# The order of twelve one-pass matmuls in a product that accumulates into two PSUM banks

## Chip, cores and metric

The kernel runs on one core of a Trainium2 chip. The time is the device time of one execution in microseconds, and the median of several executions is compared. TensorE is called PE in the profile, its weight loads PEld, VectorE DVE, ScalarE ACT, GpSimd POOL and SyncE SP. Matmul results go to PSUM, which has eight banks; a bank holds 512 fp32 values in each of 128 partitions.

## The reference

A linear attention block is followed by a two-layer feed-forward block with the gate serf(h) = h * erf(softplus(h)). Shapes: batch 8, 8 heads, sequence 576, head dimension 64; so 4608 tokens of width 512, and a hidden width of 2048.

```python
kv = np.einsum('bhsd,bhse->bhde', k, v)
out = np.einsum('bhsd,bhde->bhse', q, kv)
rms = np.sqrt(np.mean(out * out, axis=-1, keepdims=True) + 1e-06)
x = out / rms * g_norm            # then (B,H,S,D) -> (B*S, H*D)
h = x @ w_in
sp = np.maximum(h, 0.0) + np.log1p(np.exp(-np.abs(h)))
g = h * erf(sp)
return g @ w_out
```

Everything is fp32.

## The kernel before

The tokens are worked on in nine groups of 512: T = 0 to 7 take 512 of a batch entry's 576 tokens each, and T = 8 takes the 64 that each of the eight has left over. The hidden width is cut into 16 units of 128 (FC = 16), and four units make a batch (BATCH = 4). All orders are written out by hand; each engine works through its own queue in program order and waits at an instruction until what it needs is there. The waits of a matmul stand on its weight load.

**Two ways of multiplying.** For T = 0 a matmul takes plain fp32, which the array does in several passes. From T = 1 on (for w_out from the last batch of T = 1 on) a product is put together from one-pass matmuls on fp32r operands. Each operand is held in three forms: form 0, the upper part ("high"); form 1, the lower part ("low"); form 2, high and low combined with a scale ("both"). The function `product` uses two banks, n_ps and m_ps. For each of four chunks k of the contraction, forms 0 and 1 are accumulated into n_ps and form 2 into m_ps. That is twelve matmuls of 128x128 weights on 512 columns: eight into n_ps, four into m_ps. The value wanted is (SHIFT - 1) * n_ps + m_ps.

**Who calls `product`.** `hidden(T, f)` forms unit f of x @ w_in. Then ScalarE copies n_ps with the factor SHIFT - 1 into h (L1036 for T = 1, L1192 later), VectorE adds m_ps (L574), and ScalarE takes the softplus of h (L1050, L1197). `result(T, b, j, ...)` forms 128 tokens' share of g @ w_out for one batch; here VectorE takes both banks into the sum e (L1129 for the first batch of a group or L569 later for n_ps, L574 for m_ps). There are 244 products: 16 + 112 from `hidden` and 116 from `result`. In one of them, the very last, n_ps is cut into two column ranges in two banks (`cuts`).

**Which banks.** `pair_of_banks` hands out the two banks. With `turns=True` it goes round three pairs out of six banks (the two of ps_h, and o0 to o3 of ps_o), so a pair is used again three products later. In T = 1, `hidden` is called with `turns=False`, because o0 to o3 hold the output sums that `project` (L655) accumulates; all 16 products of T = 1 use the same two banks of ps_h. A tile in a bank can be written when the last reader of the tile before it there is done.

**The work around it in T = 1** (128.8 to 222.6 us). After a unit's product, four fp32 matmuls of `project` for the unit five before (LAG = 5) are issued, if there is one due: not between the first two units of T = 1, and not after the last three. In between stand pieces of attention for T = 2 (at_ps, L411 to L464). VectorE also makes the lower forms of the weights (w_lower, L561 and L564) from upper forms that ScalarE made (L558), multiplies gates (L902), and SP stores the weights' forms to DRAM. After the sixteenth product `held_sums` (L918, L949) finishes the last four units with products on o_ps and n_ps.

**The work from T = 2 on** (from 234.6 us). Each batch is four `hidden` products, then four `result` products for the batch before. The weights' forms come from DRAM (w_in_parts, w_out_parts). ScalarE makes the upper form of the gate (cut_upper, L534), and VectorE the other two in two halves of the tokens (cut_lower: L537 low, L540 both): half 0 after the first `hidden` of the next batch, half 1 after its fourth. Softplus, erf, the gate's multiplication (L1246) and one pair of heads' attention for the next group are spread over the batch. In the last batch there are only four `result` products.

Of the kernel before, what the change touches and what calls it, by code (L numbers as in the profile page):

```python
# [68 lines left out]
def kernel(  # L69
# [10 lines left out]
    nc = tc.nc  # L80
# [104 lines left out]
    def one(tiles, f):  # L185
        return tiles[f // 2][:, f % 2]

    def blocks_of(x):
        return x.rearrange("p (c f) -> p c f", c=KC)
# [102 lines left out]
    def w_next(what):  # L292
        i = w_at[what]
        if i < len(w_order):
            w_at[what] = i + 1
            {"load": load_w, "split": w_split, "join": w_join}[what](*w_order[i][1:])

    def weights():

        w_next("split")  # L300
        w_next("join")
        w_next("load")
# [275 lines left out]
    def pair_of_banks(*names, turns=True):  # L578
        pair = tuple(
            pool.tile([P, G], FP32, name=name, tag=tag)  # L580
            for name, (pool, tag) in zip(names, banks[:2])
        )
        if turns:
            banks.extend(banks[:2])
            del banks[:2]
        return pair

    def product(weights, moving, turns=True, cuts=()):


        n_ps, m_ps = pair_of_banks("n_ps", "m_ps", turns=turns)
        runs = [(n_ps, (0, 1), slice(0, G)), (m_ps, (2,), slice(0, G))]
        if cuts:
            n_ps = (n_ps, pair_of_banks("n_ps", "m_ps")[0])
            runs = runs[1:] + [(ps, (0, 1), cols) for ps, cols in zip(n_ps, cuts)]
        for ps, forms, cols in runs:
            for k in range(4):
                for form in forms:
                    nc.tensor.matmul(  # L599
                        ps[:, cols],  # L600
                        lhsT=weights(form, k),
                        rhs=moving(form, k)[:, cols],
                        start=(form == forms[0] and k == 0),
                        stop=(form == forms[-1] and k == 3),
                    )
        return n_ps, m_ps

    w_kept, w_new, w_now, w_held, w_places = {}, {}, {}, {}, {}
# [32 lines left out]
    def hidden(T, f, turns=True):  # L641

        w = w_now["in", f].pop(0).rearrange("p i (c f) -> p i c f", c=KC).bitcast(FP32R)
        x = x_forms[T]
        return product(lambda form, c: w[:, form, c], lambda form, c: x[form][:, c], turns)
# [330 lines left out]
    for n in range(FIRST * FC + 1):  # L976
# [31 lines left out]
        elif T < FIRST:  # L1008
# [11 lines left out]
            for i, c in blocks:  # L1020
                nc.tensor.matmul(  # L1021
                    plain[i],
                    lhsT=blocks_of(one(w_in_sb, i % FC))[:, c],
                    rhs=xT[T][:, c, :],
                    start=(c == 0),
                    stop=(c == KC - 1),
                )
        if T < FIRST:
# [22 lines left out]
            if n == FC - 2:  # L1051
# [8 lines left out]
                forms = late.tile([P, 3, KC, G], FP32R, name="x_forms0")  # L1060
# [57 lines left out]
    def result(T, b, j, g, w, cuts=()):  # L1118

        ps = product(  # L1120
            lambda form, f: g[j // 2][:, form, f, j % 2 * P : j % 2 * P + P],
            lambda form, f: w[f][:, form],
            cuts=cuts,
        )
        if b == 0:
            if j == 0:
                all_e = wide.tile([P, J, DM], FP32, name="e", tag="a")
                es.update((i, all_e[:, i]) for i in range(J))
            nc.vector.tensor_scalar(  # L1129
                out=es[j], in0=ps[0], scalar1=SHIFT - 1.0, scalar2=None, op0=ALU.mult  # L1130
            )
        elif not cuts:
            add_scaled(es[j], ps[0], SHIFT - 1.0)
        add(es[j], ps[1])
        for n_ps, cols in zip(ps[0], cuts):
            add_scaled(es[j][:, cols], n_ps[:, cols], SHIFT - 1.0)
            store(T, j, es[j], cols)
# [5 lines left out]
    for m in range(first_batch, batches + 1):  # L1143
# [3 lines left out]
        if T + 1 < NG:  # L1147
            todo = list(attention(T + 1, b, in_parts=last_))
            if b == 0:
                side = late_r if T % 2 == FIRST % 2 else late  # L1150
                forms = side.tile([P, 3, KC, G], FP32R, name=f"x_forms{(T + 1) % 2}")
# [73 lines left out]
        for j in range(J):  # L1225
            cuts = (slice(0, 3 * P), slice(3 * P, DM)) if m == batches and j == J - 1 else ()
# [59 lines left out]
```

## Time and profile before

| What | Value |
|---|---|
| Median of 3 runs | 902.89 us (902.69 to 903.44) |
| Span of the profiled execution, first to last instruction | 901.3 us |
| PE busy | 893.6 us, 99% |
| DVE busy | 766.7 us, 85% |
| ACT busy | 595.1 us, 66% |
| Granted TensorE clock | 0.999 |
| Matmuls of L599 into n_ps, from T = 2 on | 1,832 of 389 to 392 ns each (mean by group) |
| Matmuls of L599 into m_ps, from T = 2 on | 912 of 389 ns each |

For the profiled execution the span is its own time; the median of the runs is 1.6 us above it. Matmuls are pipelined: a row of 389 ns overlaps the next one, so the distance from start to start counts, not the length. In a timeline, the first column is the start in us from the span's start, the second the length, and in brackets stands how long the engine was idle before and what ended that. A run of like instructions stands in one row with its count. A list of waits gives who waited for whom: us in total, times, and the longest.

### The profile page before, as it was taken

What the parts mean: (1) busy time and instruction counts of PE and PEld (TensorE: products, weight loads), DVE (VectorE), ACT (ScalarE), POOL (GpSimd) and SP (SyncE); (2) the same over time, 40 slices, a digit from 0 to 9 for tenths busy, and PEclk for the clock granted to TensorE, in tenths of its full rate; (3) what the DMA queues carried; (4) which work ended last, traced back from release to release, by engine and by line L of the source; (5) the groups of instructions that cost most, each with busy time, mean ns of one, the idle gap of its engine ahead of it and who ended that gap; (6) DMA issues with size and microseconds to landing.
All of it is one profiled execution on the core that took longest, in us unless ns stands there. A gap on an engine that the chain in (4) does not pass through costs nothing.

```text
span 901.3 us, 13468 instructions
## 1 busy us (share of the span) xinstructions
PE 893.6 (99%) x4962; PEld 672.4 (75%) x4962; DVE 766.7 (85%) x1105; ACT 595.1 (66%) x789; POOL 4.7 (1%) x14
## 2 busy tenths in 40 slices
PE   8999999999999999999999999999999999999998
PEld 4444456666788888888888888888888888888887
DVE  5899978899799888888888888888888888886667
ACT  5976687777766666666766666666666666665552
POOL 2000000000000000000000000000000000000000
PEclk9999999999999999999999999999999999999999
DMA  9977418899699987988899979988897787778871
GB/s 285 295 224 226 108 73 319 305 341 355 233 384 355 347 301 258 382 308 297 273 361 336 320 248 335 365 300 292 286 341 273 270 304 309 286 282 323 317 263 51
DMA packets 136929, 259.89 MB, mean 288 GB/s; under 512 B 78816, under 2 KB 87264, under 8 KB 136864
## 3 DMA queue, kind: packets, MB, share of 16 engines
q1 hardware_dynamic: 136128, 258.09, 81.3%
q8 instruction: 39, 0.64, 0.3%
q10 hardware_dynamic: 544, 0.82, 0.3%
q14 instruction: 26, 0.21, 0.1%
q0 software_dynamic: 192, 0.13, 0.0%
HBM read 224.40 MB, written 34.60 MB: 287 GB/s over the span
## 4 chain that ended last, share of the span: by engine, by line
PE 96%; DMA 1%; DVE 1%; ACT 1%; issue 0%; SPq 0%; DVEq 0%
PE n_ps L599 50%; PE m_ps L599 25%; PE o_ps L655 9%; PE h_ps L1021 5%; PE at_ps L425 2%; PE at_ps L411 2%; PE n_ps L918 1%; PE at_ps L463 1%; PE at_ps L464 1%; DMA q_sb<-in_q_dram 1%; DMA w_raw<-in_moe_w_out_dram 1%; PE o_ps L918 0%; DVE w_e L276 0%; PE o_ps L722 0%; DVE w_in_sb L281 0%; PE ms_ps L729 0%
## 5 line engine op out<-in xcount | busy, mean ns | idle before, releaser
L599 PE MATMUL n_ps<-w_out_parts,g_forms 128*128 128x512 f32 (+1 forms) x936 | 230.7, 389 | 0.0
L599 PE MATMUL n_ps<-x_forms,w_in_parts 128*128 128x512 f32 x896 | 223.9, 392 | 0.0
L599 PEld LDWEIGHTS n_ps<-w_out_parts,g_forms 128*128 128x128 f32 x936 | 173.7, 188 | 35.3
L599 PEld LDWEIGHTS n_ps<-x_forms,w_in_parts 128*128 128x128 f32 x896 | 166.6, 188 | 35.3
L574 DVE TENSOR_TENSOR h<-m_ps,h 128x512 f32<-128x512 f32 x116 | 78.2, 687 | 60.3 <-PE m_ps L599 58.1
L599 PE MATMUL m_ps<-w_out_parts,g_forms 128*128 128x512 f32 x464 | 124.0, 389 | 0.0
L599 PE MATMUL m_ps<-x_forms,w_in_parts 128*128 128x512 f32 x448 | 119.7, 389 | 0.0
L1192 ACT ACTIVATE h<-n_ps 128x512 f32<-128x512 f32 x112 | 66.2, 594 | 75.1 <-PE n_ps L599 75.0
L1197 ACT ACTIVATE s<-h 128x512 f32<-128x512 f32 x112 | 68.3, 629 | 70.0 <-DVE h L574 70.0
L599 PEld LDWEIGHTS m_ps<-w_out_parts,g_forms 128*128 128x128 f32 x464 | 87.1, 188 | 18.5
L599 PEld LDWEIGHTS m_ps<-x_forms,w_in_parts 128*128 128x128 f32 x448 | 84.1, 188 | 17.5
L574 DVE TENSOR_TENSOR e<-m_ps,e 128x512 f32<-128x512 f32 x116 | 80.2, 692 | 15.2 <-PE m_ps L599 5.3
L655 PE MATMUL o_ps<-w_out_sb,h_sb 128*128 128x512 f32 x192 | 86.8, 595 | 0.0
L540 DVE SCALAR_TENSOR_TENSOR g_forms<-g_forms 128x1024 fp32r<-128x1024 f32 x58 | 71.1, 1225 | 2.0
L537 DVE TENSOR_TENSOR g_forms<-h,g_forms 128x1024 fp32r<-128x1024 f32 x58 | 70.6, 1217 | 1.2 <-ACT g_forms L534 1.1
L534 ACT ACTIVATE g_forms<-h 128x1024 fp32r<-128x1024 f32 x58 | 58.4, 1049 | 15.5 <-PE m_ps L599 11.1
L569 DVE SCALAR_TENSOR_TENSOR e<-n_ps,e 128x512 f32<-128x512 f32 (+1 forms) x89 | 60.4, 678 | 6.9 <-PE n_ps L599 6.9
L1246 DVE TENSOR_TENSOR h<-h,s 128x1024 f32<-128x1024 f32 x56 | 65.9, 1218 | 0.0
L655 PEld LDWEIGHTS o_ps<-w_out_sb,h_sb 128*128 128x128 f32 x192 | 35.5, 190 | 38.3 <-issue 36.9
L1021 PE MATMUL h_ps<-xT,w_in_sb 128*128 128x512 f32 x128 | 57.9, 596 | 1.1 <-DVE w_in_sb L281 1.1
L115 ACT ACT_TABLE_LOAD x43 | 55.2, 1283 | 0.8
L1220 ACT ACTIVATE s<-s 128x1024 f32<-128x1024 f32 x50 | 50.6, 1053 | 0.3
(148 smaller groups left out, 1018.7 us busy)
## 6 DMA issues: line engine op xcount, KB each, us to landing
w_out_parts<-w_out SPq DMA_DIRECT2D x116, 768.0 KB, 6.8
w_in_parts<-w_in SPq DMA_DIRECT2D x112, 768.0 KB, 6.7
w_in<-w_new SPq DMA_DIRECT2D x16, 768.0 KB, 4.9
k_sb<-in_k_dram SPq DMA_DIRECT2D x32, 288.0 KB, 5.9
v_sb<-in_v_dram SPq DMA_DIRECT2D x31, 288.0 KB, 5.8
w_raw<-in_moe_w_in_dram SPq DMA_DIRECT2D x16, 512.0 KB, 5.9
w_raw<-in_moe_w_out_dram SPq DMA_DIRECT2D x8, 1024.0 KB, 5.1
out_dram<-e SPq DMA_DIRECT2D x32, 256.0 KB, 3.8
```

Of the source, the lines that this page charges most:

```text
L115: nc.scalar.preload_act_table_set("softplus")
L534: nc.scalar.activation(high, x, AF.Copy, scale=1.0 + 2.0**-13)
L537: nc.vector.tensor_tensor(out=low, in0=x, in1=high.bitcast(FP32), op=ALU.subtract)
L540: nc.vector.scalar_tensor_tensor(out=both, in0=low.bitcast(FP32), scalar=SHIFT, in1=high.bitcast(FP32), op0=ALU.mult, op1=ALU.add,)
L569: nc.vector.scalar_tensor_tensor(out=out_, in0=ps, scalar=scale, in1=out_, op0=ALU.mult, op1=ALU.add)
L574: nc.vector.tensor_tensor(out=out_, in0=ps, in1=out_, op=ALU.add)
L599: nc.tensor.matmul(ps[:, cols], lhsT=weights(form, k), rhs=moving(form, k)[:, cols], start=(form == forms[0] and k == 0), stop=(form == fo ...
L655: nc.tensor.matmul(o_ps[j], lhsT=g[:, j * P : j * P + P], rhs=one(w_out_sb, f), start=(f == 0), stop=last,)
L1021: nc.tensor.matmul(plain[i], lhsT=blocks_of(one(w_in_sb, i % FC))[:, c], rhs=xT[T][:, c, :], start=(c == 0), stop=(c == KC - 1),)
L1192: nc.scalar.activation(h[:, i], n_ps, AF.Copy, scale=SHIFT - 1.0)
L1197: nc.scalar.activation(s[:, i], h[:, i], AF.Softplus)
L1246: nc.vector.tensor_tensor(out=part(h, half), in0=part(h, half), in1=part(s, half), op=ALU.mult)
```

## The change

The twelve matmuls of a product are put in another order. Before, the eight matmuls into n_ps come first (for each chunk form 0, form 1), then the four into m_ps. After, each chunk k has its three together: form 0 into n_ps, form 2 into m_ps, form 1 into n_ps. The operands, the banks, the start and stop marks and the number of matmuls stay as they are. A product with `cuts` keeps its order. Forms 0 and 1 of neighbouring chunks still follow each other in n_ps.

```diff
-        for ps, forms, cols in runs:
-            for k in range(4):
-                for form in forms:
-                    nc.tensor.matmul(
-                        ps[:, cols],
-                        lhsT=weights(form, k),
-                        rhs=moving(form, k)[:, cols],
-                        start=(form == forms[0] and k == 0),
-                        stop=(form == forms[-1] and k == 3),
-                    )
+        order = [(*run, k, form) for run in runs for k in range(4) for form in run[1]]
+        if not cuts:
+            order.sort(key=lambda one_: (one_[3], (0, 2, 1)[one_[4]]))
+        for ps, forms, cols, k, form in order:
+            nc.tensor.matmul(
+                ps[:, cols],
+                lhsT=weights(form, k),
+                rhs=moving(form, k)[:, cols],
+                start=(form == forms[0] and k == 0),
+                stop=(form == forms[-1] and k == 3),
+            )
         return n_ps, m_ps
```

## The prediction

> **What bounds the kernel now.** I read the page first (parts 1, 2, 4), then the list of what PE (TensorE) waits for, then timelines by engine, and last the starts of single matmuls.
>
> ```profile
> PE 893.6 (99%) x4962; PEld 672.4 (75%) x4962; DVE 766.7 (85%) x1105; ACT 595.1 (66%) x789; POOL 4.7 (1%) x14
> PEclk9999999999999999999999999999999999999999
> PE 96%; DMA 1%; DVE 1%; ACT 1%; issue 0%; SPq 0%; DVEq 0%
> ```
>
> TensorE is the bound: 96% of the chain that ended last, clock granted in full throughout. So there are two ways to move the time: another distance from matmul to matmul, or a wait on TensorE that isn't there now. Today there is next to none; its longest waits over the whole span are
>
> ```profile
> PE warm_ps L802 <- DVE ones L198: 1.4, 1, 1.4
> PE h_ps L1021 <- DVE w_in_sb L281: 1.1, 2, 0.7
> ...
> PE n_ps L918 <- ACT e L949: 0.2, 1, 0.2
> ```
>
> (total us, times, longest). Only the third lies after 128 us, where the changed products begin. A saving on DVE (VectorE) or ACT (ScalarE) would bring nothing; a delay there costs as soon as it reaches a bank or an operand that TensorE wants.
>
> **Distance between matmuls.** The change makes more neighbours differ in bank. The trace already holds both kinds side by side, in PE's timeline:
>
> ```profile
> 226.80 1.07 PE L918 MATMUL o_ps<-w_place,g_held 128*128 128x512 f32 x4
> 227.70 1.07 PE L918 MATMUL n_ps<-w_place,g_held 128*128 128x512 f32 x4
> 228.61 1.07 PE L918 MATMUL o_ps<-w_place,g_held 128*128 128x512 f32 x4
> 229.52 1.07 PE L918 MATMUL n_ps<-w_place,g_held 128*128 128x512 f32 x4
> ```
>
> The o_ps rows are four matmuls into four different banks, the n_ps rows two pairs, each pair into one bank. Start to start: 0.90, 0.91, 0.91 us for four, about 227 ns each, either way. In the starts of single matmuls after 258 us, an m followed by the next n takes 226.8 ns on average (178 pairs), an n followed by its m 226.9 (219), an m by an m 227.0 (661). A change of bank is free and brings nothing. Now to the count: of the 11 neighbourings inside a product one changes bank today (n8 to m1), 8 would afterwards (n m n n m n n m n n m n). 243 products are reordered, 7 x 243 = 1,701 neighbourings in all. The rows leave at most 1 ns on each, so 0 us, with bounds of -1.7 and +1.7. I take 0.
>
> Here two rules of the Trainium skill bear. "TensorE: Matmul & The Clock Gate", section "Back-to-back issue gap", gives N/2.4 + 2.5 ns, which is 216 ns for 512 columns, below the 227 of the rows. If that gap of about 11 ns were the price of one bank, an estimate by the page would be 1,701 x 11 = 18.7 us gained and 888 us; the page names no such cause, and the switching rows above show 227 too.
>
> **What moves: the end of n.** Today the eight n matmuls end 0.93 us before the four m matmuls. After the change n's last matmul is the product's twelfth and m's last the eleventh. ACT's copy of n (0.60 us) then starts 0.93 us later, and DVE's add of m (0.69), which needs that copy, begins when the copy ends: 0.6 us later than now wherever it waited for TensorE. In the result products DVE reads both banks itself; there the pair ends up to 0.87 us later. Second, m's first matmul moves from place 9 to place 2: its bank and its third operand (the "both" form) are wanted 1.6 us earlier.
>
> "Perfetto Trace Analysis", section "Matmuls", of the skill says that groups should rotate through banks so that the evacuation of one overlaps the matmuls of the next. Read strictly it speaks against this change: the copy of n lies under m's matmuls today and would lie under nothing of its own product. By that rule alone, exposed in each of 243 products, an estimate is 243 x 0.60 = 146 us. The rows decide where it is exposed.
>
> *Where banks don't rotate (16 products, 128.8 to 222.6 us).* They all use the same two banks (turns=False). Behind 12 of them stand 3.4 us of projection matmuls (o_ps L655), behind one 1.3 us of attention matmuls, behind the last 2.5 us of means and held sums: enough for 0.04 + 0.60 + 0.06 + 0.69 = 1.39 us of copy and add. Behind the products at 128.82 and 216.78 the next one follows at once:
>
> ```profile
> 131.06 1.09 PE L599 MATMUL m_ps<-x_both,w_new 128*128 128x512 f32 x4
> 131.99 0.42 PE L599 MATMUL n_ps<-x_high,w_new 128*128 128x512 f32 x1
> 132.24 0.40 PE L599 MATMUL n_ps<-x_low,w_new 128*128 128x512 f32 x1
> 132.47 0.39 PE L599 MATMUL n_ps<-x_high,w_new 128*128 128x512 f32 x1
> ```
>
> ```profile
> 131.26 0.60 ACT L1036 ACTIVATE h_sb<-n_ps 128x512 f32<-128x512 f32 x1 [0.76 <-PE n_ps L599]
> 132.25 0.69 DVE L574 TENSOR_TENSOR h_sb<-m_ps,h_sb 128x512 f32<-128x512 f32 x1 [2.72 <-PE m_ps L599]
> ```
>
> Today the copy ends at 131.86, under m's matmuls, and the next product's n starts at 131.99 unhindered. Afterwards: the product ends at 132.15, copy 132.19 to 132.79, add 132.85 to 133.54. The next product's first matmul must wait for the copy, its second (now m) for the add. A weight load that waited starts 0.05 us after its release and its matmul takes 0.11 us more than the usual 0.227 (copy end 230.77, matmul 230.82, next one 231.16). So the third matmul starts at 133.54 + 0.05 + 0.227 + 0.11 = 133.93 and not 132.47: 1.46 us. The other place is the same to 0.01 us (219.63, third at 220.12, then 221.57): 1.45 us. Together 2.9 us, all on the path.
>
> For the rest of this stage the nearest margins, from end of add to start of the second matmul of the next product, are 0.76 us (product at 212.19), 1.07 (205.95) and 1.23 (179.08). The first shrinks by 0.6 to 0.15. In the others a chain of ACT work in front (uppers, softplus, Ln, Exp, table loads) hands on the full 0.93 us, leaving 0.14 and 0.30. Cost 0; if I am wrong by 0.2 us on each, 0.5 us in all. What queues on DVE behind a later add (gates, w_lower and its DMAs on SP) serves the product after the next and has over 2 us.
>
> *The entry to the rotating stage.* The first product at 234.58 takes banks that held n_ps[2] and n_ps[3] of the held sums:
>
> ```profile
> 234.58 2.01 PE L599 MATMUL n_ps<-x_forms,w_in_parts 128*128 128x512 f32 x8
> 234.78 0.60 ACT L949 ACTIVATE e<-n_ps 128x512 f32<-128x512 f32 x1 [0.69 <-PE n_ps L918]
> 236.42 1.08 PE L599 MATMUL m_ps<-x_forms,w_in_parts 128*128 128x512 f32 x4
> ```
>
> The copy of n_ps[3] ends at 235.37; m wants that bank at 236.42 today, at 234.81 afterwards. Third matmul at 235.37 + 0.05 + 0.34 = 235.76, not 235.03: 0.73 us.
>
> *Rotating stage (227 products, three pairs).* A bank is wanted again three products (8.2 us) later. Margins from add to the second matmul three products on: 1.72 us once per ordinary batch, least 1.09 (product at 776.91). The shift of DVE, 0.6 to 0.87, fits in each, and it doesn't pile up: in the batch from 353.8 to 377.6 DVE idles 2.2 us, 1.34 of it in front of the fourth h add, where it waits for TensorE again and is back in step. Cost 0.
>
> *The last batch.* DVE works without a gap from 875.58, so the 0.59 us stays to the end:
>
> ```profile
> 890.24 1.22 DVE L540 SCALAR_TENSOR_TENSOR g_forms<-g_forms 128x1024 fp32r<-128x1024 f32 x1
> 891.63 1.98 PE L599 MATMUL n_ps<-w_out_parts,g_forms 128*128 128x512 f32 x8
> ```
>
> The third form is finished at 891.46, then at 892.05. Today it is used at place 9 (893.45); afterwards at place 2 (891.86). Third matmul at 892.05 + 0.05 + 0.34 = 892.44, not 892.09: 0.35 us. What follows (cut product, last store) is bound by TensorE and moves along.
>
> **Sum.** 1.46 + 1.45 + 0.73 + 0.35 = 4.0 us. The profiled execution spans 901.3 us, 1.6 below the median of 902.89; 905.3 of span gives 906.9 us.
>
> **Rivals.**
> 1. *Same bank costs something that single changes don't show* (the other side). If neighbours in one bank came down from 226.7 to the shortest distance of any pair in the trace, 224 ns, 1,701 x 2.7 = 4.6 us would come off: 906.9 - 4.6 = 902.3, no slower than now. It decides from 2.4 ns on each (4.0/1,701); to be faster by over 0.2% it takes 3.4 ns. For: 230 to 239 ns between the n matmuls of some products of the two-bank stage. Against: the four-bank rows at 227. 11%, of which 5% faster by over 0.2%.
> 2. *DVE falls behind in the rotating stage.* If its 0.87 us reached TensorE in each of 28 batches: 24 us, 931 us; if a third of it, 8 us, 915 us. For: DVE is busy 20.7 of 23.8 us in the batch from 330. Against: margins of 1.09 and more at each bank. 9%.
> 3. *TensorE's new waits are made good later*, because something else was late anyway. It could only be at 230.82, where TensorE now loses 0.4 us to ACT: 906.5. But that copy itself waits for TensorE (n_ps L918). 5%, inside the range.
>
> The forecast has 75%; with rival 3 that is 8 in 10. Range 904.9 to 909.0: below for 1.7 us of distance and 0.3 of noise, above for 1.7 and the 0.5 of thin margins. About what this kernel's measurement tells from no change is 0.2%, 1.8 us. Faster by more: 0.05, from rival 1. Within it: 0.08, the rest of rival 1 and 2% of the forecast's own lower edge. Slower: 0.87.
>
> **What would show it.** Right: waits of PE on DVE h_sb and h L574 at about 133 and 221 us, on ACT e L949 at 235, on DVE g_forms L540 at 892; 227 ns between matmuls elsewhere; DVE's idle time in front of the fourth h add of a batch shorter in total, never zero. Wrong: products of other than 2.72 us in the rotating stage (rival 1), or waits of PE on L574 or L569 once per batch (rival 2).

## The result, and the profile after

The median after the change is 906.56 us (906.46 to 906.95, 4 runs) against 902.86 us before (902.69 to 903.44, 4 runs: the three of the table above and one timed beside the new kernel): 1.0041 times as long, 95% interval 1.0028 to 1.0053. The change costs 3.7 us. The profiled execution took 906.61 us and spans 904.8 us, 3.5 more than before.

Parts 1, 2 and 4 of the page after:

```profile
span 904.8 us, 13218 instructions
...
PE 895.1 (99%) x4962; PEld 672.9 (74%) x4962; DVE 766.0 (85%) x1105; ACT 598.1 (66%) x789; POOL 4.7 (1%) x14
...
PEclk9999999999999999999999999999999999999999
...
PE 94%; DMA 2%; DVE 1%; SPq 1%; ACT 0%; issue 0%; DVEq 0%
```

TensorE is still the bound, with the same 4962 matmuls at full clock; DVE's busy time has not grown. What is new stands at the end of the list of PE's waits (its last six rows; total us, times, longest):

```profile
PE n_ps L600 <- ACT h_sb L1037: 0.7, 1, 0.7
PE n_ps L600 <- ACT h L1037: 0.7, 1, 0.7
PE m_ps L600 <- ACT e L950: 0.5, 1, 0.5
PE n_ps L919 <- ACT e L950: 0.2, 1, 0.2
PE m_ps L600 <- DVE h_sb L574: 0.2, 1, 0.2
PE m_ps L600 <- DVE h L574: 0.2, 1, 0.2
```

All but the fourth row, which is in the list of before too, are new. (Lines behind the change are one higher than before: L1037 is ScalarE's copy of n, L950 its copy of a held sum. L574, DVE's add of m, stands ahead of the change and keeps its number.) PE's timeline at the first place shows how one product hands over to the next:

```profile
131.70 0.39 PE L600 MATMUL n_ps<-x_low,w_new 128*128 128x512 f32 x1
132.77 0.50 PE L600 MATMUL n_ps<-x_high,w_new 128*128 128x512 f32 x1 [0.69 <-ACT h_sb L1037]
133.50 0.50 PE L600 MATMUL m_ps<-x_both,w_new 128*128 128x512 f32 x1 [0.23 <-DVE h_sb L574]
133.84 0.40 PE L600 MATMUL n_ps<-x_low,w_new 128*128 128x512 f32 x1
```

The two readers, in the timelines of ACT and then DVE:

```profile
132.12 0.60 ACT L1037 ACTIVATE h_sb<-n_ps 128x512 f32<-128x512 f32 x1 [1.72 <-PE n_ps L600]
```

```profile
132.75 0.69 DVE L574 TENSOR_TENSOR h_sb<-m_ps,h_sb 128x512 f32<-128x512 f32 x1 [3.31 <-ACT h_sb L1037]
```

The copy starts only when the whole product is over and ends at 132.72; n's next matmul starts 0.05 us later. The add ends at 133.44; m's next matmul starts 0.06 us later. The entry to the rotating stage, in PE's timeline and then ACT's:

```profile
237.17 0.39 PE L600 MATMUL n_ps<-x_forms,w_in_parts 128*128 128x512 f32 x1
238.02 0.50 PE L600 MATMUL m_ps<-x_forms,w_in_parts 128*128 128x512 f32 x1 [0.46 <-ACT e L950]
```

```profile
237.37 0.60 ACT L950 ACTIVATE e<-n_ps 128x512 f32<-128x512 f32 x1 [0.69 <-PE n_ps L919]
```

The copy of the last held sum ends at 237.97, and the m matmul that wants its bank starts at 238.02. The last batch, in PE's timeline and then DVE's:

```profile
894.72 0.61 PE L600 MATMUL n_ps<-w_out_parts,g_forms 128*128 128x512 f32 x2
895.25 0.50 PE L600 MATMUL m_ps<-w_out_parts,g_forms 128*128 128x512 f32 x1
895.58 0.63 PE L600 MATMUL n_ps<-w_out_parts,g_forms 128*128 128x512 f32 x2
```

```profile
893.97 1.23 DVE L540 SCALAR_TENSOR_TENSOR g_forms<-g_forms 128x1024 fp32r<-128x1024 f32 x1
```

The third form is done at 895.20 and the m matmul that wants it starts at 895.25. This wait is missing from PE's list and stands in the list of the weight loads:

```profile
PEld m_ps L600 <- DVE g_forms L540: 0.3, 1, 0.3
```

**The ledger.** Matmuls stand in both traces in issue order, so the start of the N-th one after, less its start before, is the delay up to there; its steps say where the time went. Steps in us, by place, for the profiled execution of every kernel ("133" and "221" are the two places where two products follow each other in the same banks, "between" the twelve products that lie between them, "rotating" from 247 to 892 us). Every execution also has an offset of its own, -0.6 to +0.3 us, before the first changed product; the steps leave it out. The rotating products alone were run a second time for their trace (e1b), because the profiled execution of e1 had a granted clock of 0.851 and took 997.95 us, against 903.45 to 904.34 us for its other ten.

| kernel | 133 | between | 221 | held sums, 224 | entry, 235 | rotating | last batch | sum |
|---|---|---|---|---|---|---|---|---|
| after | 1.46 | 0.03 | 1.42 | -0.22 | 0.72 | -0.01 | 0.20 | 3.6 |
| e2_two_banks_only | 1.43 | 0.02 | 1.41 | -0.21 | 0.00 | 0.00 | 0.00 | 2.6 |
| e1b_rotating_only | 0.00 | 0.00 | 0.00 | 0.00 | 0.72 | -0.01 | 0.21 | 0.9 |
| e5_no_bank_waited | 0.0 | 0.0 | 0.0 | 0.0 | 0.0 | 0.0 | 0.0 | 0.0 |
| e6_old_17_31 | 0.93 | 0.02 | 0.91 | -0.26 | 0.73 | -0.01 | 0.26 | 2.6 |
| e7_old_16_30 | 0.86 | 0.03 | 1.18 | -0.21 | 0.72 | -0.01 | 0.22 | 2.8 |
| e8_cover | 0.62 | 0.05 | 1.44 | -0.21 | 0.72 | -0.01 | 0.22 | 2.8 |
| e10_six_old | 0.05 | 0.03 | 0.08 | 0.23 | 0.01 | 0.00 | 0.00 | 0.4 |
| e3_n_n_m | 1.02 | 0.13 | 0.96 | -0.22 | 0.49 | 0.00 | 0.02 | 2.4 |
| e4_m_first | 0.93 | -0.41 | 0.93 | -0.25 | 0.00 | 0.07 | 0.45 | 1.7 |
| e9_m_n_n | 1.43 | 0.05 | 1.41 | -0.22 | 0.73 | -0.01 | 0.48 | 3.9 |

### The profile page after: what moved, and what is told of

Read it like the earlier page. It is cut to its first block, busy times and chain, and to the rows that moved or that the text cites. A ratio compares the mean times of both kernels' runs of the same rounds, so it can differ in the third digit from the quotient of the medians.

```text
span 904.8 us, 13218 instructions
## 1 busy us (share of the span) xinstructions
PE 895.1 (99%) x4962; PEld 672.9 (74%) x4962; DVE 766.0 (85%) x1105; ACT 598.1 (66%) x789; POOL 4.7 (1%) x14
## 4 chain that ended last, share of the span: by engine, by line
PE 94%; DMA 2%; DVE 1%; SPq 1%; ACT 0%; issue 0%; DVEq 0%
PE n_ps L600 50%; PE m_ps L600 25%; PE o_ps L656 9%; PE h_ps L1022 5%; PE at_ps L425 2%; PE at_ps L411 2%; DMA w_raw<-in_moe_w_out_dram 1%; PE n_ps L919 1%; DMA w_raw<-in_moe_w_in_dram 1%; PE at_ps L463 1%; PE at_ps L464 1%; SPq L143 1%; PE o_ps L919 0%; DMA q_sb<-in_q_dram 0%; DVE w_e L276 0%; SPq L149 0%
## 5 line engine op out<-in xcount | busy, mean ns | idle before, releaser
L600 PE MATMUL n_ps<-w_out_parts,g_forms 128*128 128x512 f32 (+1 forms) x936 | 294.2, 389 | 0.0
L600 PE MATMUL n_ps<-x_forms,w_in_parts 128*128 128x512 f32 x896 | 286.0, 392 | 0.0
L600 PEld LDWEIGHTS n_ps<-w_out_parts,g_forms 128*128 128x128 f32 x936 | 175.1, 188 | 36.1
L600 PEld LDWEIGHTS n_ps<-x_forms,w_in_parts 128*128 128x128 f32 x896 | 168.2, 188 | 35.9
L600 PE MATMUL m_ps<-w_out_parts,g_forms 128*128 128x512 f32 x464 | 180.3, 390 | 0.0
L600 PE MATMUL m_ps<-x_forms,w_in_parts 128*128 128x512 f32 x448 | 174.6, 390 | 0.5 <-ACT e L950 0.5
L574 DVE TENSOR_TENSOR h<-m_ps,h 128x512 f32<-128x512 f32 x116 | 78.1, 687 | 64.5 <-ACT h L1193 63.3
L600 PEld LDWEIGHTS m_ps<-w_out_parts,g_forms 128*128 128x128 f32 x464 | 87.1, 188 | 18.0 <-DVE g_forms L540 0.3
L600 PEld LDWEIGHTS m_ps<-x_forms,w_in_parts 128*128 128x128 f32 x448 | 84.1, 188 | 17.6 <-ACT e L950 0.9
L574 DVE TENSOR_TENSOR e<-m_ps,e 128x512 f32<-128x512 f32 x116 | 80.1, 691 | 4.0
```

The costliest lines, as they stand in the source:

```text
L574: nc.vector.tensor_tensor(out=out_, in0=ps, in1=out_, op=ALU.add)
L600: nc.tensor.matmul(ps[:, cols], lhsT=weights(form, k), rhs=moving(form, k)[:, cols], start=(form == forms[0] and k == 0), stop=(form == fo ...
```

## The experiments

Two theories were set against each other. **W**: the time is made of waits at four places (133, 221, 235 and 892 us), where a bank or an operand is wanted earlier than its last reader or writer is done; elsewhere the order is free. **P**: each of the 1,701 additional changes of bank costs about 2.2 ns (3.7 us / 1,701), so the time goes with the number of reordered products. Every experiment starts from the kernel after; `product` counts its calls (i from 0: products 0 to 15 use the two banks that don't rotate, 16 is the first of the rotating stage, 240 to 243 are the last batch) by

```diff
+    made = []
...
+        made.append(0)
+        i = len(made) - 1
```

which moves L600 to L604, L1037 to L1041 and L950 to L954. The medians ("before beside it" is the kernel before, timed together with that run):

| kernel | us | before beside it | ratio | 95% interval |
|---|---|---|---|---|
| e1_rotating_only | 904.11 | 903.02 | 1.0009 | 1.0000 to 1.0018 |
| e2_two_banks_only | 905.87 | 903.02 | 1.0027 | 1.0016 to 1.0039 |
| e3_n_n_m | 905.27 | 903.02 | 1.0022 | 1.0014 to 1.0031 |
| e4_m_first | 905.03 | 903.02 | 1.0021 | 1.0012 to 1.0029 |
| e5_no_bank_waited | 902.95 | 902.78 | 1.0001 | 0.9993 to 1.0010 |
| e6_old_17_31 | 905.74 | 902.78 | 1.0029 | 1.0018 to 1.0041 |
| e7_old_16_30 | 906.11 | 902.78 | 1.0033 | 1.0020 to 1.0045 |
| e8_cover | 905.74 | 902.78 | 1.0030 | 1.0019 to 1.0042 |
| e9_m_n_n | 906.79 | 902.80 | 1.0045 | 1.0029 to 1.0060 |
| e10_six_old | 903.34 | 902.80 | 1.0006 | 0.9998 to 1.0015 |
| e1b_rotating_only, one execution | 904.13 | | | |

### One stage alone

```diff
-        if not cuts:
+        if not cuts and turns:
```

> New order only in the 227 products of the rotating stage; the 16 products on two banks keep the old order. Theory W (the time is lost in waits for a bank or for the third form, at four places, and a change of bank costs nothing): the waits at the entry (0.73 us) and in the last batch (0.19 us in the trace after) stay, those at 133 and 222 us go: 0.9 us over the kernel before. Rival P (each change of bank costs a little: 3.7 us over 1,701 changes, 2.2 ns each): 227 of 243 products keep the cost, 3.5 us over the kernel before.

```diff
-        if not cuts:
+        if not cuts and not turns:
```

> New order only in the 16 products on two banks. Theory W: two waits of 1.48 us come, 0.26 us is given back in the held sums (a wait on g_held there falls away when TensorE is late): 2.6 us over the kernel before. Rival P: 16 of 243 products, 0.2 us over.

The 16 products that don't rotate bring +2.85 us, the 227 that do +1.09, as W has it; by P it would be the other way round (0.2 and 3.5). The same kernel once more, for its trace:

> The first experiment's kernel again, for its trace: between the last batch and the end of the stage on two banks nothing but the entry's 0.73 us and the last batch's 0.2 us; a start of the first rotating product neither earlier nor later than before.

Its span is 902.4 us, 1.1 more than before, and its ledger has the two steps of the rotating part at its ends and nothing in 645 us between. The two halves (2.6 + 0.9) make up the whole (3.6).

### Only products that no bank waits for

```diff
-        if not cuts:
+        if not cuts and 16 < i < 240:
```

> New order in 223 products, in which no wait is expected: all of the rotating stage but its first product and the last batch. Theory W: 0 us against the kernel before (within 0.4). Rival P: 223 of 243 products, 3.4 us over.

223 of the 243 products are reordered, and the time is that of before: +0.17 us, interval -0.07% to +0.10%. After its own offset of -0.6 us the ledger stays level within 0.05 us over 223 x 7 = 1,561 additional changes of bank: 0.03 ns on each. P is ruled out, and so is its opposite, that a change of bank gains something. The whole list of PE's waits, with nothing new in it:

```profile
PE warm_ps L807 <- DVE ones L198: 1.4, 1, 1.4
PE h_ps L1026 <- DVE w_in_sb L281: 1.1, 2, 0.7
PE o_ps L727 <- ACT qT L724: 0.9, 1, 0.9
PE n_ps L923 <- ACT e L954: 0.2, 1, 0.2
```

### The two halves of the wait at 133 and 221 us

First the later product of each pair in the old order, so that m is wanted at place 9 again:

```diff
-        if not cuts:
+        if not cuts and i not in (1, 15):
```

> New order everywhere but in the second and the last product on two banks, the two that had to wait. Theory W: they still wait for the copy of n at their first matmul, but no longer for the add at their second: 0.94 us at each place and not 1.48, so 1.0 us less than the changed kernel, 2.5 us over the kernel before. Rival P: as the changed kernel, 3.7 us over.

Then the earlier one, so that its copy lies under its own m matmuls again:

```diff
-        if not cuts:
+        if not cuts and i not in (0, 14):
```

> New order everywhere but in the first and the last but one product on two banks, the two whose banks are waited for. Theory W: the copy of n is on time again, the second matmul of the next product waits for the add, which starts 0.5 us earlier than in the changed kernel: 0.87 us at each place and not 1.48, so 1.2 us less than the changed kernel, 2.3 us over the kernel before. Rival P: as the changed kernel, 3.7 us over.

PE's waits on the pair of banks, first in e6 and then in e7:

```profile
PE n_ps L604 <- ACT h_sb L1041: 0.7, 1, 0.7
PE n_ps L604 <- ACT h L1041: 0.7, 1, 0.7
```

```profile
PE m_ps L604 <- DVE h L574: 0.8, 1, 0.8
PE m_ps L604 <- DVE h_sb L574: 0.6, 1, 0.6
```

Each half alone costs 0.9 us and both together 1.46. They add up only in part, for the copy and the add are one chain: in e6 TensorE waits for the copy alone and the add is done by the time it is wanted; in e7 the copy is done in time, and the add is not. Undoing one side saves 0.5 to 0.6 us of the 1.46. The second place in e7 misses W's figure, 1.18 us instead of 0.87; in the wait list that is 0.8 instead of 0.6. DVE's timeline of e7 shows why. These are the adds of product 13 and of product 14 (the first of the pair at 221 us):

```profile
216.88 0.69 DVE L574 TENSOR_TENSOR h<-m_ps,h 128x512 f32<-128x512 f32 x1 [0.41 <-ACT h L1041]
...
220.90 0.68 DVE L574 TENSOR_TENSOR h<-m_ps,h 128x512 f32<-128x512 f32 x1
```

Product 13 is in the new order, so its copy ends later and its add starts 0.54 us later than before (216.88 against 215.67, less the 0.67 us by which all of e7 runs late there). From that add to the next one DVE works without an idle time that could take up the delay, and product 14's add starts 0.33 us late (220.90 against 219.90), although its copy had ended at 220.25 and its last m matmul at 220.47. In the kernel after, the same queue is done 0.21 us before the later copy lets the add go (221.86), so nothing of it shows.

### Cover between the two products

The last of the four `project` matmuls of the step before (output group J-1) is issued behind the first product instead of in front of it (`project` takes the output groups to work on as a new last argument; its definition is not shown here):

```diff
-                project(f + FC - LAG, hs[n - LAG], False)
+                project(f + FC - LAG, hs[n - LAG], False, range(J - 1))
...
+            if f == 0:
+                project(f + FC - LAG, hs[n - LAG], False, (J - 1,))
```

> The changed kernel, with one of the four output sums of the extra projection in front of the first two-bank product issued behind it (two passes of 0.43 us). Theory W: 0.86 us of work then lies between the first and the second product, so the wait of 1.48 us there shrinks to 0.62, the other stays: 0.86 us less than the changed kernel, 2.8 us over the kernel before. Rival P: as the changed kernel, 3.7 us over.

```profile
131.18 1.02 PE L660 MATMUL o_ps<-w_out_sb,h_sb 128*128 128x512 f32 x2
132.03 0.50 PE L604 MATMUL n_ps<-x_high,w_new 128*128 128x512 f32 x1
132.76 0.50 PE L604 MATMUL m_ps<-x_both,w_new 128*128 128x512 f32 x1 [0.23 <-DVE h_sb L574]
```

PE's timeline at 133 us: the 0.85 us of moved work (131.18 to 132.03) lies under the copy, the wait on L1043 (this kernel's copy) is gone at this place, that on the add remains. The step falls from 1.46 to 0.62, the expected figure; the second place, left alone, keeps 1.44. The price was the lack of work between two products, and not the order in itself.

### All but six products

```diff
-        if not cuts:
+        if not cuts and i not in (0, 1, 14, 15, 16, 242):
```

> New order in 237 products; the old one only in the six at the four places: the first two and last two on two banks, the first of the rotating stage and the third of the last batch. Theory W: these six carry the whole loss, so 0 us against the kernel before (within 0.4). Rival P (2.2 ns for each change of bank): 237 of 243, 3.6 us over.

237 products in the new order cost +0.5 us by the medians (interval -0.02% to +0.15%) and 0.4 by the ledger. Six products carry the rest. More than half of the 0.4 is one step at the held sums; PEld's waits there in e10, and those of the kernel before:

```profile
PEld o_ps L923 <- DVE g_held L540: 0.6, 1, 0.6
```

```profile
PEld o_ps L918 <- DVE g_held L540: 0.4, 1, 0.4
```

Here TensorE arrives as early as before (222.88 us in both), but DVE ends the held gate that it waits for at 224.07 instead of 223.85. The delay is the one of e7: the add of product 13, in the new order here too, starts at 216.12 instead of 215.67, and DVE again works on without idling. So these 0.2 us are a price of the new order that the change itself does not pay, because TensorE is 2.85 us late there by its other waits.

### Other orders, and which bank is whose

Both n forms of a chunk, then its m:

```diff
-            order.sort(key=lambda one_: (one_[3], (0, 2, 1)[one_[4]]))
+            order.sort(key=lambda one_: (one_[3], one_[4]))
```

> Per chunk n, n, m instead of n, m, n: 7 instead of 8 changes of bank per product, n ends at place 11 and m at 12, m starts at place 3. Theory W: the copy of n starts one matmul earlier and the bank of m is wanted one matmul later, so 1.0 us at each of the two places, 0.5 at the entry, 0 in the last batch, 0.2 given back: 2.3 us over the kernel before. Rival P: six sevenths of 3.7, 3.2 us over. The distance on DVE from the n_ps to the m_ps row of a result product, 0.79 us before and 0.72 after, is back at 0.79 if it depends on which bank is finished last.

W's figure came (median +2.25, ledger 2.4, for 2.3), and not the 3.2 us that 7 changes of bank in 11 neighbourings, against 8 in the change, would have cost by P. n ends one matmul sooner and m is wanted one later: 1.46 - 2 x 0.227 = 1.01 at 133 us (1.02 measured), and at the entry 0.72 - 0.23 = 0.49 (0.49).

All four m first:

```diff
-            order.sort(key=lambda one_: (one_[3], (0, 2, 1)[one_[4]]))
+            order.sort(key=lambda one_: one_[4] != 2)
```

> All four m matmuls, then all eight n: one change of bank per product, as in the kernel before, but n ends at place 12 and m starts at place 1. Theory W: the first matmul of the next product waits for the add: 1.65 us at each of the two places, 0.95 at the entry, 0.4 in the last batch, some 0.2 at two thin margins of the two-bank stage, 0.3 given back: 4.5 us over the kernel before, more than the changed kernel. Rival P: no more changes of bank than before, so 0 us over.

Both theories miss: +2.0 us. In PE's timeline of e4, and then in DVE's:

```profile
133.12 1.19 PE L604 MATMUL m_ps<-x_both,w_new 128*128 128x512 f32 x4 [0.69 <-ACT h_sb L1041]
```

```profile
133.10 0.69 DVE L574 TENSOR_TENSOR h_sb<-m_ps,h_sb 128x512 f32<-128x512 f32 x1 [3.28 <-ACT h_sb L1041]
```

m's matmuls begin at 133.12, while DVE is still reading the m of the product before until 133.79. So they are not in that bank: m has the bank that the copy freed. A theory **F** follows: the two banks are handed out in the order in which they are first written, and the one freed first goes to the tile written first. The estimate of W, in which m waited for the add of the old m, had assumed fixed names. One run tests F, with m at place 1 and n at place 2:

```diff
-            order.sort(key=lambda one_: (one_[3], (0, 2, 1)[one_[4]]))
+            order.sort(key=lambda one_: (one_[3], (1, 2, 0)[one_[4]]))
```

> Per chunk m, n, n, so m is written first and n ends at place 12. In the run with all m first, the first m matmul of the second product began while the add of the old m bank still ran. Theory F (the two banks are given out in the order of first writing, the one with the earlier last reader first): m takes the bank that the copy frees, n at place 2 the one that the add frees: 1.4 us at each of the two places, as in the changed kernel; no wait at the entry's first matmul, 0.7 us at its second; 0.4 us in the last batch; 0.2 given back: 3.7 us over the kernel before. Rival (m keeps m's bank): its first matmul waits for the add, 1.65 us at each place and 0.95 at the entry: 4.5 us over.

The median is +4.0 us, between the two figures and nearer to F's, the ledger's 3.9 likewise. PE's timeline decides:

```profile
132.80 0.50 PE L604 MATMUL m_ps<-x_both,w_new 128*128 128x512 f32 x1 [0.69 <-ACT h_sb L1041]
133.53 0.51 PE L604 MATMUL n_ps<-x_high,w_new 128*128 128x512 f32 x1 [0.23 <-DVE h_sb L574]
```

Now m waits for the copy of the old n, and n for the add of the old m. F holds. The first step equals that of the change (1.43), because the bank that is freed last is wanted at place 2 either way. The 0.28 us that this order costs more lies in the last batch, where the third form is wanted still one place earlier.

None of these versions is faster than the kernel before; the two whose intervals leave room for no change (e5, e10) bring the new order only where TensorE waits for nothing new, or, in e10, for 0.2 us.

## Why the prediction was right

The forecast was slower, 906.9 us; 906.56 came, by the predicted path. By its steps:

- **Distance 0: right.** Starts of single matmuls after the change lie 227 ns apart in the median, n to m and m to n (973 pairs each) and n to n (913). e5 shows the same by the time, which takes rival 1 and theory P away. The estimate of 888 us that a gap of 11 ns would have meant is contradicted: the trace keeps 227 ns where the formula of the Trainium skill ("TensorE: Matmul & The Clock Gate", "Back-to-back issue gap"), which the page gives for an isolated matmul, would have 216.
- **133 and 221 us: right**, 1.46 and 1.42 for 1.46 and 1.45. The prediction named only the add as the releaser to look for; in the list 0.7 us of each wait stands on the copy and 0.2 on the add. The chain is the one of the working, ending with the add, and the 0.34 us from a matmul whose weight load waited to the next one came as taken (133.50 to 133.84).
- **Thin margins in the two-bank stage: right at 0**, 0.03 us over twelve products, but partly by luck. The prediction held that what queues on DVE behind a later add serves the product after the next and has over 2 us. The queue also holds the next product's own add: behind product 13 (the one at 212.19) that add comes 0.3 us late in e7 and e10 (above). In the change the longer waits at 221 us cover it.
- **Entry: right**, 0.72 for 0.73.
- **Rotating stage: right at 0.** The delay is 3.31 us at 247 and at 891 us, and over 261.7 to 695 us no wait of PE or PEld on a bank is in the list. Rival 2 is out. The rule of the skill's "Perfetto Trace Analysis", "Matmuls", asks that the evacuation of one group lie under the next group's matmuls. With three pairs in turn it still does after the change, so the strict reading (146 us), which wanted the copy of n under its own product, went beyond the rule and did not come true; where one pair serves two products and nothing lies between, the trace bears the rule out.
- **Last batch: right in kind, too big**, 0.20 for 0.35. The term had the third form 0.59 us later than the shift of the whole program; it was 0.43 (895.20 against 891.46, less 3.31). DVE's rows show where the 0.16 went: its delay beyond the 3.31 us is 0.56 at the two pairs of reads that start at 886.20 and 887.60 before, and 0.42 behind them, since each pair became 0.07 us shorter (below). The wait on g_forms, named as a sign, is in the list of the weight loads only.
- **Missed: 0.22 us given back at the held sums.** Rival 3 had the mechanism, but said that it could only be at 230.82. It was at 223: before, eight o_ps matmuls took 2.07 us there, with the wait on g_held shown above, and after they take 1.84 (before, then after):

```profile
222.88 2.23 PE L918 MATMUL o_ps<-w_place,g_held 128*128 128x512 f32 x8
224.95 1.31 PE L918 MATMUL n_ps<-w_place,g_held 128*128 128x512 f32 x5
```

```profile
225.74 2.01 PE L919 MATMUL o_ps<-w_place,g_held 128*128 128x512 f32 x8
227.58 1.98 PE L919 MATMUL n_ps<-w_place,g_held 128*128 128x512 f32 x8
```

 This was in the trace of before, among the waits of the weight loads; the prediction had read the list of the matmuls alone.
- **Missed: DVE's idle time in front of the h adds did not shrink.** In 258 to 692 us before and 261.7 to 695 us after, from the two lists of waits:

```profile
DVE h L574 <- PE m_ps L599: 26.4, 32, 1.3
```

```profile
DVE h L574 <- ACT h L1193: 30.5, 36, 1.3
```

 The releaser changes from TensorE to the copy, as it should, but DVE waits longer and not less, having saved time elsewhere. It touches no bank in time and costs nothing.

Sum: 1.46 + 1.42 + 0.72 + 0.20 - 0.22 = 3.58 us for 4.0 predicted; the 0.4 between is the last batch (0.15) and the held sums (0.22), but for 0.04. (The terms that the prediction gives for its upper bound add up to 909.1 us, not 909.0.)

**Open.** In the two-bank stage single distances of 225 to 240 ns occur; with all m first (e4) twelve products got 0.41 us shorter, with the order of the change 0.03 longer. No run says why, nor what sets each execution's own offset before the first changed product.

## What to carry to other kernels

Where matmuls already follow at a fixed distance (227 ns here, into one bank or two), the order of banks in the stream was worth nothing; what an order set was when each bank's last matmul ended and when it was first written again. So look for the few places where banks do not rotate and no other work lies between two groups: six products of 243 made nearly all of this loss. Read the waits of the weight loads as well as of the matmuls, since a wait that is already there absorbs part of a new one (0.22 us here). Undoing the long waits one by one can also lay bare a short one that they covered, as in e7 and e10.

## What the runs showed of the hardware that was not expected

- **DVE's two reads of a result product lie closer together when the second bank is finished first.** DVE's row on n_ps and the one on m_ps start 0.79 us apart before and 0.72 after, and 0.79 in e3, where m is again the last to end (medians). Pairs from DVE's timelines of before and after:

```profile
369.32 0.68 DVE L1129 TENSOR_SCALAR e<-n_ps 128x512 f32<-128x512 f32 x1
370.11 0.69 DVE L574 TENSOR_TENSOR e<-m_ps,e 128x512 f32<-128x512 f32 x1
```

```profile
373.19 0.68 DVE L1130 TENSOR_SCALAR e<-n_ps 128x512 f32<-128x512 f32 x1
373.90 0.69 DVE L574 TENSOR_TENSOR e<-m_ps,e 128x512 f32<-128x512 f32 x1
```

 The trace has 13,468 instructions before and in e3, and 13,218 after. Of the 250 fewer, 243 are waits that stand as instructions of their own on DVE's queue in front of the add of m, one for each product that is reordered. In the trace the add into e has two waits before, for DVE's own read of n and for m's matmuls, and after only the first; one of two waits is an instruction of its own. The list of L574 of the kernel before has the 243, that of after has none:

```profile
L574 DVEq EVENT_SEMAPHORE  x243: 21/21/21, 132.2 to 894.9; - x122
```

 The short distance goes with the missing wait: e5, with 223 products reordered, has 223 of these waits fewer, 112 pairs at 0.72 us, and the three of the last batch, left in the old order, at 0.79. That the wait instruction itself takes the 0.07 us is likely but not shown.
- **Banks go by first writing, not by name** (e4, e9); this is the program's allocation, but an order of matmuls changes it without a word in the code.
